# A row-lookup table moved from memory into SBUF, filled by one-hot matrix products instead of four-byte scatters

## The chip, the cores and the metric

The kernel runs on one core of a Trainium2 chip, in one launch. The metric is the device time of the whole program in microseconds (us); lower is better. A core has five engines with queues of their own. TensorE does the matrix products: PE in the profile, and PEld for the loads of its weights. VectorE (DVE), ScalarE (ACT) and GpSimd (POOL) do the rest, and SyncE (SP) only issues DMA transfers. Each engine works through its own list strictly in the order in which the program wrote it, so an instruction that waits holds up everything written behind it on that engine. SBUF is the memory on the core, PSUM the eight banks into which TensorE writes, and "memory" without a name is the chip's HBM, reached by DMA alone.

## The reference

The reference is a linear attention with two mixture-of-experts blocks behind it:

```
phi(x): p = x @ w_phi; p -= max|p|; [exp(p), exp(-p)]
attention: num = phi(q) @ (phi(k)^T v); den = phi(q) @ sum(phi(k)); num / den
block 1:   logits = x @ w_gate + bias[modality]; e = argmax; g = softmax(logits)[e]
           out = g * (relu(x @ w1[e]) @ w2[e])
block 2:   the same without the bias, and times sigmoid(x @ w_output_gate)[e]
```

There are 8 batches of 8 heads with 576 positions of 64 numbers, so 4608 rows of 512 numbers go through both blocks. Each block has 8 experts with 512 x 1024 and 1024 x 512 weights, and a row goes to one expert only.

## The kernel before, in words

**Rows and places.** A row can reach its expert only once its logits are known, so the kernel sorts rows by expert as it goes. Every finished row is written to a list in memory (`x1_d` for block 1; the code counts it as block 0). The row's place in the order of its expert is its expert's number times 4608 plus its rank among the rows of that expert so far. A table with one entry per place (8 x 4608 = 36,864 entries) says which row stands there. Later, a tile of 128 consecutive places is looked up in the table, and its 128 rows are fetched by one indirect DMA (`gather`, L749).

**The table.** It lies in memory, in five copies `tab0_0` to `tab0_4` of four-byte entries (L71), zeroed in the attention stage (`zeros`, L436). For each 128 rows `enter` (L364) issues one indirect DMA on POOL that scatters 128 entries of four bytes. Block 1 of the code (the second block of experts) has four such copies and the same `enter`.

**The attention stage.** A loop of 78 steps (L1560) treats one group of heads of one batch per step, nine steps to a batch; this text calls nine steps a period and numbers its steps 0 to 8. A step works on several batches at different stages, so that products of TensorE lie beside maxima and differences on DVE and exponentials on ACT. `weave` holds chains of small DVE instructions, from which a step takes a few at fixed points. Within a step, TensorE gets in this order: projections (`proj`, L1205), `q_less` (L1340), `kv_head` (L1297), `num` (L1382), then for rows that are nearly done `x_logits` (L376) and `a_T` (transposes, L371). `num` has one PSUM bank. Before the next `num` can write, DVE must have taken the last one out (`norm`, L1362 to L1366).

A batch's rows are stored (`x_store`), ranked on TensorE (`x_ranks`), placed on DVE (`x_places`) and entered (`x_enter`, L1529) while the loop works two periods further on. This falls in steps 6 to 8 of the period; batches with an odd number come a step later than those with an even number, and go into the table at step 0 of the next period. Even batches have 4 tiles of 128 rows here, odd ones 5.

**The turn to the experts.** The expert with most rows in the first six batches begins early. `early_rows` (L557) reads three tiles of table entries for it by DMA on SP, `early_idx` (L567) adds up the five copies on DVE, and three gathers follow. The last two batches are finished behind the loop, between the first products of the experts (`tiles()`). Then `route_a` (L614) reads the whole table into SBUF on SP, works out on DVE which tile goes to which expert, and `route_b` (L691) looks up the rows of the other 40 tiles by 30 products with a selection matrix (5 copies x 2 halves x 3 parts, L699). Memory that the attention's last rows used is used again by `route_a`; it must wait for their store.

**The experts.** 40 tiles per block, two layers per tile (`first`, L782 to L784; `second`, L802 to L806), weights loaded by SP. The rows of block 1 enter its own table four tiles at a time.

Of the kernel before, what the change touches and what calls it, by code (L numbers as in the profile page):

```python
# [53 lines left out]
def attention_two_moe(  # L54
# [13 lines left out]
    x2_d = dpool.tile([NSLOT * 128 + 1, XW], F32, name="x2_d")  # L68
    rows_of = [C1 * 128, NSLOT * 128]

    tab_d = [[dpool.tile([NROW, 1], F32, name=f"tab{n}_{k}") for k in range(K)] for n, K in enumerate((5, G))]  # L71

    whole = ((0, 1),)

# [36 lines left out]
    row_no = []  # L111
    for n in range(2):
# [6 lines left out]
        row_no.append(t.rearrange("p c t -> p (c t)").bitcast(F32))  # L119

    nxt = [iota(f"nxt{n}", [[NT, NE]]) for n in range(2)]
    row0 = iota("row0", [[NT, NE]])
# [219 lines left out]
    def places(ps, oh16, C, n, valid=None):  # L342

        pl = sp.tile([128, CM, NE], F32, tag="pl", name="pl")[:, 0:C]
        nc.vector.tensor_tensor(
            pl, ps[:, 0:C], nxt[n].unsqueeze(1).to_broadcast([128, C, NE]), op=ALU.add)
        nc.vector.tensor_tensor(nxt[n], nxt[n], ps[:, C], op=ALU.add)
        yield
        nc.vector.tensor_tensor(pl, pl, oh16[:, 0:C], op=ALU.mult)
        yield  # L350
        po = sp.tile([128, CM], F32, tag="po", name="po")[:, 0:C]
        nc.vector.tensor_reduce(out=po, in_=pl, op=ALU.add, axis=AX.X)
        yield
# [8 lines left out]
        return pi  # L362
# [155 lines left out]
    etab = [const.tile([128, len(tab_d[n]), E], F32, name=f"etab{n}") for n in range(2)]  # L518
    ereg = {}

    def early(n):
# [45 lines left out]
    def early_idx(n):  # L567
        s = sp.tile([128, E, 2], F32, tag="es", name="es")
        nc.vector.tensor_reduce(
            out=s, in_=etab[n].rearrange("p k c -> p k c").bitcast(F16).rearrange("p k (c t) -> p c t k", t=2),  # L570
            op=ALU.add, axis=AX.X)
        yield
        nc.vector.scalar_tensor_tensor(
            out=s[:, :, 1], in0=s[:, :, 0], scalar=128.0, in1=s[:, :, 1], op0=ALU.mult, op1=ALU.add)
        yield
        nc.vector.tensor_scalar(eidx[n], s[:, :, 1], float(rows_of[n]), None, op0=ALU.add)
        yield
# [12 lines left out]
    def rt(n, name, shape, dt=F32, keep=False):  # L590
        if (n, name) not in rts and keep:
            rts[n, name] = const.tile(shape, dt, name=f"{name}{n}")
        elif (n, name) not in rts:
            words = int(np.prod(shape[1:])) * (2 if dt == F16 else 4) // 4
            area = next((a for a in spare if a[1] + words <= a[2]), None)
            if shape[0] == 128 and n == 0 and area:
                rts[n, name] = view(area[0], dt, area[1] * (2 if dt == F16 else 1), *shape[1:])
                area[1] += words
            elif n == 1 and (0, name) in rts:
                rts[n, name] = rts[0, name]  # L600
            else:
                rts[n, name] = state["late"].tile(shape, dt, tag=name, name=name)
        return rts[n, name]
# [87 lines left out]
    def route_b(n):  # L691


        tab16, sel, ntile, ex = routed[n, "a"]
        rows = state["pg"][:, 3, 0 : 2 * M].rearrange("p (t m) -> p t m", t=2)
        for x in range(2):
            for i, t in enumerate(tab16):
                for k in range(3):
                    nc.tensor.matmul(  # L699
                        rows[:, x], t[:, k, :, x], sel[:, k], start=(i == 0 and k == 0),  # L700
                        stop=(i == len(tab16) - 1 and k == 2))
        rs = rt(n, "rs", [128, M])
        nc.vector.tensor_scalar(rs, rows[:, 0], 128.0, float(rows_of[n]), op0=ALU.mult, op1=ALU.add)
        idx = rt(n, "idx", [128, M], I32, True)
        nc.vector.tensor_tensor(idx, rs, rows[:, 1], op=ALU.add)
# [412 lines left out]
    with ExitStack() as actx:  # L1118
# [405 lines left out]

        def x_places(b):
            n = 4 + b % 2
            rows[b, "pi"] = yield from places(rows[b, "rk"], rows[b, "oh"], n, 0)

        def x_enter(b):  # L1529
            pi = rows.pop((b, "pi"))  # L1530
            for c in range(4 + b % 2):
                enter(0, pi, c, 9 * (b // 2) + 4 * (b % 2) + c)

        def x_store(b):
            for c, r in rows[b]:
# [19 lines left out]
        def tiles():  # L1555
            if not chains.get("route"):
                chains["route"] = next(experts)

        chains = {}
        for t in range(9 * B + 6):  # L1560
            b, s = t // 9, t % 9

            def at(lag, n=9):

                u = t - lag
                return (u // 9, u % 9) if 0 <= u < 9 * B and u % 9 < (n if n else 4 + u // 9 % 2) else None
# [35 lines left out]
            if b + 2 < B and s in (5, 6):  # L1602
                load_qk(q_of(b + 2), qT[b + 2], s - 5)
            split_step(split0, weave, t, "load")
            ready = batch_at(23)
            if ready != B - 3:
                ready = batch_at(24)
                ready = None if ready == B - 3 else ready
            if ready is not None:
                weave.finish(chains.pop(("finish", ready)))  # L1610
                x_store(ready)
# [54 lines left out]
            for x in firsts[t][1:] if 4 <= t < 9 else []:  # L1666
                proj(q_proj(*x))
                q_max(*x)
            each(5, num)
            if at(18, 0) and at(18)[0] < B - 1:  # L1670
                x_logits(*at(18))
            if at(17, 0) and at(17)[0] < B - 1:
                a_T(*at(17))
            if ready is not None:
                x_ranks(ready)
                chains["places", ready] = weave.add(x_places(ready))
# [18 lines left out]
            entered = ready if ready == B - 3 else batch_at(26)  # L1695
            if entered is not None and (entered, "pi") in rows:
                x_enter(entered)
# [6 lines left out]
            if t == 9 * B + 1:  # L1704
                done(early_idx(0))
                for i in range(E):
                    gather(0, i)
            if t in (9 * B + 1, 9 * B + 5):
# [41 lines left out]
        x_enter(last)  # L1750


    late = ctx.enter_context(tc.tile_pool(name="late", bufs=1))
# [85 lines left out]
```

## Time and profile before

| what | us |
|---|---|
| three runs: median (lowest to highest) | 1561.77 (1560.21 to 1566.68) |
| the profiled execution's own time | 1563.24 |
| its span, first to last instruction | 1561.5 |
| PE busy | 1467.9 (94%) |
| DVE busy | 746.4 (48%) |
| ACT busy | 553.4 (35%) |
| POOL busy | 228.3 (15%) |

The span is cut into 40 slices of 39 us; in the rows below a digit is the busy share of a slice in tenths, and PEclk is the granted clock of TensorE in tenths of 2.4 GHz. The attention stage takes slices 0 to 13, the two blocks of experts the rest. A wait named "issue" is one in which the profile shows nothing that the engine waited for.

### The profile page before, as it was taken

How to read it: one execution, taken by the hardware profiler on the slowest of the kernel's cores; microseconds unless marked ns; L12 is line 12 of the kernel's file. 1: busy time of each engine (PE TensorE's matmuls, PEld its weight loads, DVE VectorE, ACT ScalarE, POOL GpSimd, SP SyncE). 2: the span in 40 equal slices, each digit the busy share in tenths (PEclk: the TensorE clock that was granted, in tenths of full speed). 3: DMA queues.
4: the chain of work that ended last, by engine and by line, in shares of the span. 5: the costliest groups of instructions: out<-in, count | busy, mean ns of one | idle time of the engine just before them, and what ended most of it. 6: DMA issues, size and time to landing. Idle time of an engine off the chain costs nothing. (4 is left out here: it accounts for less than half of the span.)

```text
span 1561.5 us, 38909 instructions
## 1 busy us (share of the span) xinstructions
PE 1467.9 (94%) x15626; PEld 1157.4 (74%) x15626; DVE 746.4 (48%) x2255; ACT 553.4 (35%) x850; POOL 228.3 (15%) x273
## 2 busy tenths in 40 slices
PE   6999998987999879999999999799889999999998
PEld 4999998987989847667777776466657777777775
DVE  3668776757756434646665666354341111111111
ACT  1346565554555403334444444243211111111111
POOL 1000101101011121202211211120131211211221
PEclk8999998989989889999999999899999999999999
DMA  8255656677431753657667777678945353484381
GB/s 250 92 159 164 142 170 157 174 168 136 124 62 49 265 84 114 158 185 201 204 213 178 195 180 230 113 199 244 306 150 174 76 150 104 133 272 138 81 281 43
DMA packets 158268, 254.40 MB, mean 163 GB/s; under 512 B 90953, under 2 KB 95613, under 8 KB 152192
## 3 DMA queue, kind: packets, MB, share of 16 engines
q1 hardware_dynamic: 141264, 210.22, 50.2%
q0 software_dynamic: 14784, 41.44, 7.9%
q8 instruction: 127, 2.08, 0.7%
q14 instruction: 61, 0.50, 0.1%
q10 hardware_dynamic: 2032, 0.16, 0.1%
HBM read 428.60 MB, written 83.22 MB: 328 GB/s over the span
## 5 line engine op out<-in xcount | busy, mean ns | idle before, releaser
L784 PE MATMUL proj<-xT,w 128*128 128x128 f16 x896 | 154.8, 221 | 10.4 <-issue 10.4
L783 PE MATMUL proj<-xT,w 128*128 128x128 f16 x896 | 154.7, 221 | 6.1 <-issue 6.1
L782 PE MATMUL proj<-xT,w 128*128 128x128 f16 x896 | 154.6, 220 | 3.2 <-issue 3.2
L802 PE MATMUL num<-w,qs 128*128 128x512 f32 x336 | 151.6, 605 | 0.0
L794 DVE SCALAR_TENSOR_TENSOR qs<-proj,qs 128x512 f16<-128x512 f32 x54 | 37.4, 692 | 228.3 <-ACT qs L793 228.3
L784 PEld LDWEIGHTS <-w 128*128 128x128 f16 x1344 | 132.2, 98 | 18.6 <-issue 18.6
L802 PE MATMUL num<-ks,qs 128*128 128x512 f32 x304 | 140.1, 614 | 4.2 <-DMA ks<-in_moe_w_dram 4.2
L1382 PE MATMUL num<-kvsb,E 128*128 128x65 f32 x1024 | 129.6, 282 | 11.9 <-DVE xt L1366 11.8
L782 PE MATMUL proj<-xT,v 128*128 128x128 f16 x816 | 138.7, 219 | 0.7 <-DVE xT L771 0.7
L784 PE MATMUL proj<-xT,v 128*128 128x128 f16 x816 | 138.7, 219 | 0.2 <-issue 0.2
L783 PE MATMUL proj<-xT,v 128*128 128x128 f16 x816 | 138.7, 219 | 0.0
L782 PEld LDWEIGHTS <-w 128*128 128x128 f16 x1344 | 132.1, 98 | 8.4 <-issue 4.4
L1382 PEld LDWEIGHTS num<-kvsb,E 128*128 128x128 f32 x1024 | 125.6, 200 | 14.9 <-issue 8.3
L1297 PE MATMUL kv<-v,kp 128*128 128x128 f32 x1024 | 135.7, 288 | 0.5 <-issue 0.5
L783 PEld LDWEIGHTS <-w 128*128 128x128 f16 x1344 | 132.1, 98 | 4.0 <-issue 2.0
L752 POOL DMA_INDIRECT xg<-x_d,idx x74 | 77.6, 1049 | 388.7 <-PE px L371 189.5
L1297 PEld LDWEIGHTS kv<-v,kp 128*128 128x128 f32 x1024 | 126.6, 201 | 1.6 <-issue 1.6
L783 PEld LDWEIGHTS <-v 128*128 128x128 f16 x1216 | 118.9, 98 | 3.1 <-issue 1.0
L782 PEld LDWEIGHTS <-v 128*128 128x128 f16 x1216 | 118.9, 98 | 2.5 <-issue 0.4
L784 PEld LDWEIGHTS <-v 128*128 128x128 f16 x1216 | 118.9, 98 | 0.0
L802 PEld LDWEIGHTS num<-w,qs 128*128 128x128 f32 x336 | 63.3, 193 | 72.0 <-issue 72.0
L1205 PE MATMUL proj<-wps,ks 64*128 64x128 f32 (+1 forms) x640 | 113.9, 301 | 0.9 <-issue 0.6
(328 smaller groups left out, 3366.7 us busy)
## 6 DMA issues: line engine op xcount, KB each, us to landing
w<-pl SPq DMA_DIRECT2D x114, 1024.0 KB
v<-pl SPq DMA_DIRECT2D x80, 1024.0 KB
ks<-in_moe_w_dram SPq DMA_DIRECT2D x40, 1024.0 KB
ks<-pl SPq DMA_DIRECT2D x40, 1024.0 KB
w<-in_moe_w_dram SPq DMA_DIRECT2D x38, 1024.0 KB
wf<-in_moe_w_dram SPq DMA_DIRECT2D x64, 512.0 KB
pl<-wo SPq DMA_DIRECT2D x52, 512.0 KB
w<-in_moe_w_dram SPq DMA_DIRECT2D x32, 512.0 KB
```

The lines of the kernel that those rows point to most:

```text
L752: nc.gpsimd.indirect_dma_start(out=xg(n, i), out_offset=None, in_=src[n][0:nr, :], in_offset=bass.IndirectOffsetOnAxis(ap=ix, axis=0), bou ...
L782: nc.tensor.matmul(h[:, j], wk[:, 0, cs], xT[:, k], start=(k == 0), stop=False)
L783: nc.tensor.matmul(h[:, j], wk[:, 0, cs], xT[:, 4 + k], start=False, stop=False)
L784: nc.tensor.matmul(h[:, j], wk[:, 1, cs], xT[:, k], start=False, stop=(k == 3))
L794: nc.vector.scalar_tensor_tensor(out=lo, in0=h, scalar=0.0, in1=hi, op0=ALU.max, op1=ALU.subtract)
L802: nc.tensor.matmul(y, h[:, k], wk, start=(k == 0), stop=(k == 7))
L1205: nc.tensor.matmul(*a, **kw)
L1297: nc.tensor.matmul(ps[:, half, h % 2], kp[:, c, half, :], vw(v1, 4 * h + c), start=(h % 2 == 0 and half == 0 and c == 0), stop=False)
L1382: nc.tensor.matmul(ps[:, c, 0:V], e[:, half, 128 * c : 128 * c + 128], kw(g, half), start=(half == 0), stop=(half == 1))
```

## The change

The table of the first block of experts becomes one tile in SBUF, `tab0`: 96 partitions x 3 x 128 entries of float16. Nothing of it goes to memory: the five copies, the DMAs that zero them, the 36 scatters, the five reads of `early_rows` and the five of `route_a` go away. The second block's tables stay as they are.

For each tile of 128 rows `hots` makes two one-hot matrices on DVE: `a` (128 x 128: the low seven bits of the place, times a code for the row's number) and `o` (128 x 288: the other bits). `tab_add` multiplies them: three products per tile, summed in one PSUM bank over the 4 or 5 tiles of a batch. `tab_out` adds the bank to `tab0`. A lookup is three products (`tab_pick`) and three DVE instructions (`decode`). In the loop, all batches up to the sixth are now ready at step 6 and entered at step 7; one-hot matrices lie in buffers borrowed from other uses. In step 1, `num` is now issued behind `x_logits` and `a_T`. `early_sel` and `tab_pick` at the steps 71 and 72 replace the reads of `early_rows`, and the early gathers come one step earlier.

```diff
+    tab0 = const.tile([96, 3, 128], F16, name="tab0")
+    nc.gpsimd.memset(tab0, 0.0)
...
+        nc.vector.tensor_scalar(pi, pi, 127, None, op0=ALU.bitwise_and)
+        nc.vector.tensor_copy(pk, pi)
+        nc.vector.tensor_tensor(po, po, pk, op=ALU.subtract)
...
+    def hots(at_, pk, po, c0, mems):
+        for c, m in enumerate(mems):
+            a, o = m[:, 0:128], m[:, 128:416]
+            nc.vector.tensor_scalar(
+                a, iota128, pk[:, c : c + 1], code[:, c0 + c : c0 + c + 1], op0=ALU.is_equal, op1=ALU.mult)
+            nc.vector.tensor_scalar(o, iota_c, po[:, c : c + 1], None, op0=ALU.is_equal)
+            out_.append((a, o))
+            yield
+    def tab_add(tag, hs_):
+        ps = bank(tag, F32, 3, 128)
+        for k in range(3):
+            for i, (a, o) in enumerate(hs_):
+                nc.tensor.matmul(
+                    ps[0:96, k], o[:, 96 * k : 96 * k + 96], a, start=(i == 0), stop=(i == len(hs_) - 1))
+    def tab_out(ps):
+        nc.vector.tensor_tensor(tab0, tab0, ps[0:96], op=ALU.add)
...
-        for k, t in enumerate(tab_d[n]):          # early_rows, route_a: n = 0 has no copies left
...
+        if n == 0:                                  # route_b
+            tab_pick(rows[:, 0], sel)
+            done(decode(idx, rows[:, 0], "bits", M))
...
-            ready = batch_at(23)
-            if ready != B - 3:
-                ready = batch_at(24)
-                ready = None if ready == B - 3 else ready
+            ready, entered = [(t - x) // 9 if (t - x) % 9 == 0 and 0 <= (t - x) // 9 < B - 2 else None for x in (24, 25)]
...
-            each(5, num)
+            if entered is not None:
+                weave.finish(chains.pop(("hots", entered)))
+                x_enter(entered)
+                tab_out(rows.pop((entered, "pt")))
+            if s != 1:
+                each(5, num)
             ...
+            if s == 1:
+                each(5, num)
...
-        x_enter(last - 1)
-        tiles()
         for c in range(n):
             x_logits(last, c)
+        done(x_hots(last - 1))
+        x_enter(last - 1)
+        tab_out(rows.pop((last - 1, "pt")))
+        tiles()
         done(finish(last))
         tiles()
         x_ranks(last)
         x_store(last)
         done(x_places(last))
-        x_enter(last)
+        done(x_hots(last))
+        x_enter(last, "num2")
+        tab_out(rows.pop((last, "pt")))
```

## Rows read from the trace of the kernel before

**Rows 1.** The page: busy time of each engine (us, share of the span, instructions).
```profile
PE 1467.9 (94%) x15626; PEld 1157.4 (74%) x15626; DVE 746.4 (48%) x2255; ACT 553.4 (35%) x850; POOL 228.3 (15%) x273
```

**Rows 2.** Windows: length, busy PE PEld DVE ACT POOL (instructions), clock, DMA share, GB/s.
```profile
133.96:191.02 57.06, 54.84 (x650) 52.52 (x646) 45.53 (x120) 33.27 (x57) 4.59 (x5) 0.97 0.66 164
191.02:248.79 57.77, 55.40 (x673) 52.28 (x670) 44.00 (x119) 35.01 (x59) 5.26 (x6) 1.00 0.67 196
248.79:311.36 62.57, 58.06 (x643) 55.01 (x643) 45.34 (x120) 32.30 (x55) 5.16 (x5) 0.92 0.61 136
311.36:377.61 66.25, 60.15 (x665) 56.94 (x663) 46.77 (x127) 34.23 (x58) 6.15 (x7) 0.90 0.68 172
377.61:442.99 65.38, 56.27 (x634) 53.45 (x633) 43.44 (x118) 33.69 (x58) 4.29 (x5) 0.90 0.60 101
442.99:453.50 10.51, 8.79 (x84) 8.31 (x82) 4.72 (x14) 4.94 (x8) 0.00 (x0) 0.84 0.08 7
```

**Rows 3.** Waits of PE, 120 to 575 us: total, times, longest.
```profile
PE num L1382 <- DVE xt L1366: 10.5, 11, 2.5
PE proj L1205 <- issue: 8.3, 4, 7.4
PE proj L783 <- issue: 6.1, 3, 4.5
```

**Rows 4.** Windows during and behind two groups of scatters, columns as in rows 2.
```profile
365.00:374.00 9.00, 9.00 (x107) 8.86 (x106) 8.63 (x30) 5.97 (x10) 3.42 (x5) 1.00 0.99 326
377.00:390.00 13.00, 6.06 (x65) 5.60 (x66) 5.21 (x13) 5.07 (x8) 0.00 (x0) 0.78 1.13 48
...
555.00:566.00 11.00, 3.87 (x57) 3.04 (x53) 5.51 (x26) 0.69 (x1) 3.58 (x4) 0.81 1.07 27
```

**Rows 5.** DMA queues, 376 to 392, then 360 to 374 us: packets, MB, share.
```profile
q8 instruction: 1, 0.02, 4.2%
...
q8 instruction: 1, 0.02, 0.4%
```

**Rows 6.** Line 365, the scatters: duration ns min/median/max, first and last start us.
```profile
L365 POOL DMA_INDIRECT tab<-row_no,pi x76: 967/974/1502, 178.3 to 1145.5; - x76
```

**Rows 7.** Window of one step 6, columns as in rows 2.
```profile
172.03:177.93 5.90, 4.99 (x50) 4.58 (x49) 5.83 (x19) 2.55 (x4) 0.00 (x0) 0.85 1.02 345
```

**Rows 8.** DVE groups by line: count, busy us, mean ns of one, idle before.
```profile
L1274 DVE TENSOR_TENSOR kd<-proj,km 128x512 f32<-128x512 f32 x72 | 49.0, 681 | 0.2
L360 DVE CAST pi<-po 128x5 int32<-128x5 f32 x4 | 0.7, 170 | 0.2
```

**Rows 9.** Line 123, a 128x128 comparison on DVE: duration ns min/median/max.
```profile
L123 DVE TENSOR_SCALAR tri<-iota,iota_p x1: 283/283/283, 13.3 to 13.3; 128x128 f16<-128x128 f32 x1
```

**Rows 10.** Timeline, turn to the experts: start, length, instruction, count, idle before.
```profile
500.79 10.80 SPq L562 DMA_DIRECT2D etab<-tab  x5
...
516.70 2.90 PE L1382 MATMUL num<-kvsb,E 128*128 128x65 f32 x16 [2.50 <-DVE xt L1366]
...
554.67 0.27 PE L339 MATMUL pl<-oh,ones 128*128 128x40 f16 x5
...
571.30 0.49 DVE L657 TENSOR_TENSOR lt<-v,v 128x320 f32<-128x320 f32 x1 [9.94 <-DMA x_d<-kvsb]
...
572.37 0.61 PE L371 MATMUL px<-ident,qs 128*128 128x128 f16 x8
572.81 7.09 PE L802 MATMUL num<-w,qs 128*128 128x512 f32 x16
...
583.67 2.91 PE L802 MATMUL num<-w,qs 128*128 128x512 f32 x3
```

**Rows 11.** Windows behind the early lookup and behind the lookup, columns as in rows 2.
```profile
517.50:531.20 13.70, 13.70 (x114) 12.96 (x114) 4.60 (x19) 3.23 (x6) 2.25 (x5) 0.50 1.02 394
582.40:589.20 6.80, 6.42 (x28) 3.21 (x29) 3.76 (x16) 0.69 (x1) 2.49 (x3) 0.50 0.86 298
```

**Rows 12.** Waits of PE, 600 to 1100 us: total, times, longest.
```profile
PE proj L784 <- issue: 9.6, 1, 9.6
```

More of the change, by code (lines that the diff above doesn't have):

```diff
@@ L69, in attention_two_moe @@
     rows_of = [C1 * 128, NSLOT * 128]
-    tab_d = [[dpool.tile([NROW, 1], F32, name=f"tab{n}_{k}") for k in range(K)] for n, K in enumerate((5, G))]
+    tab_d = [[dpool.tile([NROW, 1], F32, name=f"tab{n}_{k}") for k in range(K)] for n, K in enumerate((0, G))]
     whole = ((0, 1),)
@@ L109, in attention_two_moe @@
     nc.gpsimd.iota(col_no, [[96, 3]], base=1, channel_multiplier=1, allow_small_or_imprecise_dtypes=True)
-    row_no = []
-    for n in range(2):
+    row_no = [None]
+    for n in (1,):
         nc_ = rows_of[n] // 128
@@ L517, in attention_two_moe @@
     eidx = [const.tile([128, E], I32, name=f"eidx{n}") for n in range(2)]
-    etab = [const.tile([128, len(tab_d[n]), E], F32, name=f"etab{n}") for n in range(2)]
+    etab = [None, const.tile([128, len(tab_d[1]), E], F32, name="etab1")]
     ereg = {}
@@ L565, in early_rows, with early_sel, tab_pick, early_idx @@
                     "e (c p) -> p (e c)", p=128))
[L567 to L572, printed above, removed]
-        nc.vector.scalar_tensor_tensor(
[L574 to L577, printed above, removed]
+    def early_sel():
+        ec = sp.tile([128, E], F32, tag="ec", name="ec")
+        nc.vector.tensor_scalar(ec, iota_m[:, 0:E], 1.0, None, op0=ALU.add)
+        nc.vector.scalar_tensor_tensor(
+            out=ec, in0=eno[0][:, 0:1].to_broadcast([128, E]), scalar=float(C1), in1=ec, op0=ALU.mult, op1=ALU.add)
+        sel = sp.tile([96, 3, E], F16, tag="esel", name="esel")
+        nc.vector.tensor_tensor(
+            sel, ec[0:96].unsqueeze(1).to_broadcast([96, 3, E]), col_no.unsqueeze(2).to_broadcast([96, 3, E]),
+            op=ALU.is_equal)
+        return sel
+    def tab_pick(ps, sel):
+        for k in range(3):
+            nc.tensor.matmul(ps, tab0[:, k], sel[:, k], start=(k == 0), stop=(k == 2))
+    def early_idx(n, ps=None):
+        if n == 0:
+            yield from decode(eidx[0], ps, "ebits", E)
+        else:
+            s = sp.tile([128, E, 2], F32, tag="es", name="es")
+            nc.vector.tensor_reduce(
+                out=s, in_=etab[n].rearrange("p k c -> p k c").bitcast(F16).rearrange("p k (c t) -> p c t k", t=2),
+                op=ALU.add, axis=AX.X)
+            yield
+            nc.vector.scalar_tensor_tensor(
+                out=s[:, :, 1], in0=s[:, :, 0], scalar=128.0, in1=s[:, :, 1], op0=ALU.mult, op1=ALU.add)
+            yield
+            nc.vector.tensor_scalar(eidx[n], s[:, :, 1], float(rows_of[n]), None, op0=ALU.add)
+            yield
         nc.vector.tensor_tensor(wes[n], winv[:, n, 0], winv[:, n, 1], op=ALU.mult)
@@ L695, in route_b @@
         rows = state["pg"][:, 3, 0 : 2 * M].rearrange("p (t m) -> p t m", t=2)
[L696 to L703, printed above, removed]
-        idx = rt(n, "idx", [128, M], I32, True)
-        nc.vector.tensor_tensor(idx, rs, rows[:, 1], op=ALU.add)
+        idx = rt(n, "idx", [128, M], I32, True)
+        if n == 0:
+            tab_pick(rows[:, 0], sel)
+            done(decode(idx, rows[:, 0], "bits", M))
+        else:
+            for x in range(2):
+                for i, t in enumerate(tab16):
+                    for k in range(3):
+                        nc.tensor.matmul(
+                            rows[:, x], t[:, k, :, x], sel[:, k], start=(i == 0 and k == 0),
+                            stop=(i == len(tab16) - 1 and k == 2))
+            rs = rt(n, "rs", [128, M])
+            nc.vector.tensor_scalar(rs, rows[:, 0], 128.0, float(rows_of[n]), op0=ALU.mult, op1=ALU.add)
+            nc.vector.tensor_tensor(idx, rs, rows[:, 1], op=ALU.add)
         nti = rt(n, "nt", [1, 1], I32, True)
@@ L1526, in x_places, with x_hots, x_enter @@
             n = 4 + b % 2
[L1527 to L1532, printed above, removed]
+            rows[b, "pk"] = yield from places(rows[b, "rk"], rows[b, "oh"], n, 0)
+        def x_hots(b):
+            n = 4 + b % 2
+            if b < B - 2:
+                areas = [wk.tile([128, 4 * F], F32, tag="kd", name="kd"),
+                         wk.tile([128, 8, 128], F16, tag="xT", name="xT", bufs=1).rearrange("p a b -> p (a b)")]
+            else:
+                areas = [io.tile([128, 4, 2, F], F32, tag="kprem", name="kprem", bufs=1).rearrange("p a b c -> p (a b c)")]
+            mems = []
+            for a in areas:
+                a = a if a.dtype == F16 else a.bitcast(F16)
+                mems += [a[:, 416 * i : 416 * i + 416] for i in range(a.shape[1] // 416)]
+            mems = mems[0:4]
+            if n == 5:
+                mems.append(sm.tile([128, 416], F16, tag="hot", name="hot", bufs=1))
+            at_ = []
+            pk, po = rows.pop((b, "pk"))
+            yield from hots(at_, pk, po, 9 * (b // 2) + 4 * (b % 2), mems)
+            rows[b, "hots"] = at_[0]
+        def x_enter(b, tag="qf"):
+            rows[b, "pt"] = tab_add(tag, rows.pop((b, "hots")))
         def x_store(b):
@@ L1694, in attention_two_moe @@
                 weave.finish(chains.pop(("places", ready)))
-            entered = ready if ready == B - 3 else batch_at(26)
-            if entered is not None and (entered, "pi") in rows:
-                x_enter(entered)
+                chains["hots", ready] = weave.add(x_hots(ready))
+                weave.step(2)
             if t == 9 * B - 3:
@@ L1703, in attention_two_moe @@
                 early_rows(0)
-            if t == 9 * B + 1:
-                done(early_idx(0))
+            if t == 9 * B - 1:
+                esel = early_sel()
+            if t == 9 * B:
+                ps = p_small[:, 384 : 384 + E]
+                tab_pick(ps, esel)
+                done(early_idx(0, ps))
                 for i in range(E):
```

26 lines of the change are left out of this document (25 added, 1 removed).

## The prediction

> **What bounds the kernel now.** I read the page first. TensorE is busy 94% of the span [rows 1], so the reader should look for time in which it is idle, or busy at half speed. I went on to windows, one for each period of nine steps in the attention stage [rows 2]. The first two take 57.06 and 57.77 us at a clock of 0.97 and 1.00. The next three do nearly the same work in 62.57, 66.25 and 65.38 us at 0.90 to 0.92. The third view, the waits of TensorE, says what the idle time is: 8.3 us before projections and 6.1 us before `first`, put down to "issue", and 10.5 us in 11 waits of `num` for DVE [rows 3].
>
> "Issue" means that no semaphore was waited for, so I looked at DMA. During one group of scatters the DMA engines moved 326 GB/s at a share of 0.99; right behind it they were as busy (1.13) and moved 48 GB/s, and behind a later group 27 GB/s at 1.07 [rows 4]. Busy engines that move little mean that single packets take long. One of those packets fetches instructions: the single fetch between 376 and 392 us took 4.2% of 16 engines x 16 us = 10.8 us, where one between 360 and 374 took 0.4% of 16 x 14 us = 0.9 us [rows 5]. TensorE then waited 7.4 us for "issue" [rows 3], and the clock fell [rows 2]. Scatters begin at 178 us [rows 6], and of the four periods behind them one is not hurt (57.77), three are [rows 2]. So I read: a group of four-byte scatters slows all DMA behind it; where an instruction fetch falls into that stretch it comes too late, TensorE stands, and then works on at a granted 0.50, 1.2 GHz [rows 11].
>
> [...]
>
> **The change part by part**, against the profiled execution of 1563.2 us (span 1561.5; 1.5 us above the median of 1561.8).
>
> *Slow DMA in the attention stage.* Three long periods against the mean of the first two (57.4): 194.2 - 172.2 = 22.0 us [rows 2]. Step 0 of the next period has 10.51 - 8.79 = 1.7 us idle and 16% of its clock missing, 1.7 us more: 3.4. All this follows scatters that go away: **-25**. If stalls have other causes, none of it goes; with the shorter waits behind it, up to -29.
>
> *Step 1.* `num` is now behind `x_logits` and `a_T`, which TensorE can do while DVE finishes `xt`. Of 10.5 us in 11 waits [rows 3], six steps 1 have about 1 us each, and 8 transposes alone take 0.61 us [rows 10]: **-4** (0 to -6). The transposed rows are ready: DVE wrote them before `xt`.
>
> *TensorE's new work.* 36 tiles x 3 products. Eight transposes of that size take 0.61 us [rows 10], 0.06 to 0.08 each: 81 in the loop and 12 behind it cost 5.2 us at 0.056 (7 at 0.076), on the path because TensorE is it: **+5**. The last 15 are in the turn, below. 30 lookup products become 3.
>
> *DVE's new work.* Per period three small instructions of 0.17 [rows 8]; per tile `a`, a 128x128 comparison (0.28, back to back some 0.2 [rows 9]) and `o`, 288 numbers: no more than 0.49, the float32 one of 320 numbers [rows 10], no less than a small one's 0.17 [rows 8]. I take 0.55 for both, between 0.35 and 0.75, as float16 from and to SBUF isn't in the trace. `tab_out` adds 384 numbers from PSUM, 0.68 for 512 [rows 8], so 0.5. Together 0.5 + 4.5 x 0.55 + 0.5 = 3.5 us a period, in steps 6 and 7. [...]
>
> DVE has 57.06 - 45.53 = 11.5 us free in a period, 1.3 a step [rows 2], but in one step 6 it is busy 5.83 of 5.90 us, and TensorE idle 0.9 [rows 7]. Odd batches now also finish and rank a step earlier, into the same step 6. What queues behind: `k_max`, `k_sub` and `norm` of the next step, and TensorE waits for these, with one bank for `num`. Two steps hide some 2 us, so 1.5 us come through, and at half clock behind part of these gaps 0.3 more: 1.8 x 6 = **+11** (0 to +30). The products of step 7 wait for `hots` themselves.
>
> *Scatters and zeros.* 36 of 76 scatters of 0.97 us leave POOL [rows 6], where they delayed nothing on the path; setup gains a memset, two iotas and four small DVE instructions and loses three, under 1 us before the first loads: 0. Five stores of zeros leave SP.
>
> *Early tiles.* The five reads of `early_rows` held SP for 10.80 us [rows 10], with the first expert weights behind them. DVE stood for them, then TensorE 2.50 us, and 16 products took 2.90 us behind it, at the lower clock. Now `tab_pick` is three products on numbers in SBUF. 2.5 go for sure. From 517.5 to 531.2 the clock is 0.50 with TensorE busy throughout [rows 11], which costs up to 6.8 us; I take half, as TensorE is little loaded just before: **-6** (0 to -9). Weights come earlier, which nothing waits for.
>
> *The turn.* Before: ranks end at 554.9; `first` is torn apart by slow fetches (4.5 us in one [rows 3]); `route_a` on DVE waits 9.94 us for the store of the last rows, to 571.30; transposes, `second` from 572.81, then the lookup, and the next product at 583.67 [rows 10]. After: behind the ranks come about eight small DVE instructions (1.5), five tiles of one-hots (2.75) and 15 products (1.1), with TensorE idle: 560.3. Then 96 products of `first` at 0.056, 5.4 us, 2 us for a lower clock, 0.6 of transposes, 7.1 of `second`, 0.6 for logits and three products: 576.0 instead of 583.7, **-7.7**. `route_a` starts 4 us later but no longer waits for a slow store. The half clock behind the lookup's wait (6.42 us busy at 0.50 [rows 11]) gives **-3.2**. Together -11 (-5 to -15).
>
> *Sum:* -25 - 4 + 5 + 11 - 6 - 11 = -30, so 1533; against the median **1532 us**. The experts of block 1 keep their 40 scatters of the other table, and one wait of 9.6 us for "issue" [rows 12]; other instruction counts shift the fetches against these slow stretches, by 10 us either way.
>
> **The rivals.**
>
> 1. *DVE absorbs the new work*, and the lower clock goes with the stalls: `o` is fast (for that speaks that free time is there on the average [rows 2], against it the full step 6 [rows 7]). Then +11 becomes +1 and the turn and the early tiles give -24: 1563.2 - 25 - 4 + 5 + 1 - 24 = 1516; with luck in the second table's stalls 1506.
> 2. *The "issue" waits aren't the scatters'.* Stores of rows share each period with them, and the fetch may be late for its own reasons; against it, full speed during the scatters and 48 GB/s right behind [rows 4]. Then -25 falls away, and of the turn only the lookup's wait goes, some 6 us, against 4 us of new wait for one-hots: 1563.2 - 4 + 5 + 11 - 6 - 2 = 1567.
> 3. *Slower: TensorE waits for `hots` in step 7 of six periods.* The other terms give 25 + 4 - 5 + 6 + 11 = 41 us, so it decides from 6.8 us a period on. Price: one-hots at 0.75 and small instructions make 4.4, the finish of odd batches adds 2, and a lower clock behind each gap 2.5, as the step behind [rows 7] at 0.85 shows it begins: 9 x 6 = 54, so 1576.
>
> **How the numbers follow.** Forecast (1517 to 1548) 0.63, rival 1 0.22, rival 2 0.07, rival 3 0.08. Range: 1504 to 1557, which takes in rival 1 and the forecast with DVE at +25; the likeliest's own is 1517 to 1548. What this kernel's runs can tell from no change is about 0.5%, 8 us. Faster by more: 0.63 + 0.22 + a little of rival 3 = 0.86; within: 0.05; slower: 0.09.
>
> **What would show it.** Right: periods of 57 to 60 us all through, GB/s that doesn't fall between 245 and 560 us, waits of TensorE for "issue" gone there, `lt` not waiting for the store, the product behind the lookup near 557 in place of 584. Step 7 shows the cost: `num` or the 96-column products waiting for DVE. Wrong: a fall of GB/s behind stores alone, or steps 6 and 7 longer by more than 6 us.

## The result, and the profile after it

| what | before | after |
|---|---|---|
| median of the runs on one chip, us | 1564.22 (1560.21 to 1567.72, 4 runs) | 1537.38 (1537.06 to 1538.08, 4 runs) |
| ratio | | 0.986 (95%: 0.981 to 0.991) |
| the profiled execution, its span | 1563.24, 1561.5 | 1537.06, 1535.2 |

The forecast was 1532 us in a range of 1504 to 1557. The time lies in it, but the sum behind it does not hold: a gain where it was forecast came out as a loss, and a part that was put at zero came out as a gain. The stages show it. Boundaries are the last `k_max` of the attention loop, the first product of `second` (first early tile), the product behind the lookup, the 65th product of `second` (two tiles later) and the 641st (the end of block 1).

| stretch of the profiled execution | before | after | difference | forecast |
|---|---|---|---|---|
| start to the last `k_max` | 499.7 | 504.7 | +4.9 | -13 (-25 - 4 + 5 + 11) |
| to the first early tile's `second` | 48.0 | 50.4 | +2.4 | -6 |
| to the product behind the lookup | 36.0 | 25.0 | -11.0 | -7.7 |
| to the 65th product of `second` | 36.7 | 34.0 | -2.7 | -3.2 |
| to the 641st | 513.2 | 489.6 | -23.6 | 0 (10 either way) |
| to the end | 427.9 | 431.6 | +3.7 | 0 |

The page, and the periods of the attention stage (length, busy PE PEld DVE ACT POOL with counts, clock, DMA share, GB/s), answer to [rows 1, 2]:

```profile
PE 1467.3 (96%) x15710; PEld 1162.3 (76%) x15710; DVE 770.2 (50%) x2365; ACT 552.4 (36%) x850; POOL 193.5 (13%) x239
```

```profile
132.07:194.70 62.63, 57.97 (x662) 54.97 (x658) 48.02 (x132) 33.14 (x57) 0.35 (x1) 0.95 0.54 167
194.70:257.61 62.91, 59.02 (x682) 55.90 (x678) 47.43 (x132) 34.55 (x59) 0.35 (x1) 0.95 0.52 162
257.61:320.94 63.33, 59.12 (x662) 55.98 (x658) 47.91 (x131) 32.47 (x56) 1.25 (x1) 0.92 0.48 149
320.94:386.67 65.73, 59.40 (x682) 56.11 (x678) 50.03 (x140) 35.35 (x59) 1.08 (x2) 0.95 0.50 155
386.67:449.75 63.08, 58.59 (x648) 55.41 (x645) 45.89 (x129) 32.37 (x57) 0.35 (x1) 0.92 0.32 100
```

All five are as long as the disturbed ones of before. The first two, which had taken 57.06 and 57.77 us, are 5 us longer. The cause is not the old one. The waits of PE in the stretch of [rows 3] have no "issue" left:

```profile
PE qf L402 <- DVE kd L394: 12.3, 10, 2.6
PE num L1460 <- DVE xt L1444: 10.3, 11, 2.5
PE num L402 <- DVE kprem L394: 2.7, 4, 2.1
PE qf L402 <- DVE xT L394: 1.6, 8, 0.2
```

The DMA rows of 240 to 560 us follow, in 40 slices of 8 us (busy share in tenths, then GB/s), first before, then after. Before, slices 9 and 10 are 7 and 8 tenths busy and move 31 and 57 GB/s, and the last is at 9 tenths and moves 67: that is the slow DMA. After, every slice of 8 or 9 tenths moves 197 GB/s or more.

```profile
DMA  9094924978765906898650076410101400899409
GB/s 306 2 123 92 250 96 150 322 31 57 187 139 132 342 16 226 289 62 71 168 146 21 2 266 116 20 66 2 66 2 48 186 2 1 308 404 397 180 2 67
```

```profile
DMA  6418651914319909332770060101102409990302
GB/s 267 147 62 214 142 205 69 348 58 139 133 52 197 311 3 316 125 97 110 202 178 5 6 261 1 68 2 66 68 2 84 152 0 334 408 388 25 120 18 96
```

What is late now is seen in one step 7, in the timeline of PE (start, length, instruction, count, idle before) and, below it, of DVE:

```profile
176.41 0.61 PE L1380 MATMUL kv<-v,kprem 128*128 128x130 f32 x4
179.60 0.26 PE L402 MATMUL qf<-kd 128*96 128x128 f16 x1 [2.58 <-DVE kd L394]
180.06 0.26 PE L402 MATMUL qf<-kd 128*96 128x128 f16 x1 [0.20 <-DVE kd L394]
...
181.41 0.28 PE L402 MATMUL qf<-xT 128*96 128x128 f16 x2
181.53 1.51 PE L1460 MATMUL num<-kvsb,E 128*128 128x65 f32 x8
```

```profile
177.54 0.41 DVE L1444 TENSOR_TENSOR xt<-num,den 128x256 f32<-128x256 f32 x1
...
179.01 0.34 DVE L392 TENSOR_SCALAR kd<-iota,pk,code 128x128 f16<-128x128 f32 x1
179.26 0.28 DVE L394 TENSOR_SCALAR kd<-iota_c,po 128x288 f16<-128x288 f16 x1
179.47 0.34 DVE L392 TENSOR_SCALAR kd<-iota,pk,code 128x128 f16<-128x128 f32 x1
...
181.73 0.55 DVE L407 TENSOR_TENSOR tab<-tab,qf 96x384 f16<-96x384 f16 x1 [0.80 <-PE qf L402]
```

The products (L402) stand ahead of `num` in TensorE's list. `num` could have started at 177.95, when `xt` was out; it starts at 181.53, and from 181.9 us on TensorE works at half clock (granted 0.50) for 6.8 us. Four of the six periods have this wait, of 2.55 to 2.58 us, the last one a shorter one (1.04); in the second 2.52 us stand ahead of `num` in the step before, where DVE is full with the odd batch (10.6 us busy in the 12.1 up to 236.56). A stretch at 0.50, of 6.8 to 13.7 us, follows each of the six.

The turn came as forecast. TensorE waits for the last one-hot matrices, `lt` on DVE starts at 573.0 us without a wait for the store, and the lookup is three products without a wait [rows 10]:

```profile
564.41 0.26 PE L402 MATMUL num<-kprem 128*96 128x128 f16 x1 [2.10 <-DVE kprem L394]
...
572.84 7.09 PE L880 MATMUL num<-w,qs 128*128 128x512 f32 x16
...
579.97 0.23 PE L636 MATMUL qf<-ks,tab 96*128 96x40 f16 x3
580.04 1.96 PE L880 MATMUL num<-w,qs 128*128 128x512 f32 x4
```

Among the experts of block 1 the wait of 9.6 us [rows 12] is gone; these are the waits of PE in the same stretch:

```profile
PE proj L861 <- issue: 1.9, 1, 1.9
PE kv L860 <- issue: 1.7, 1, 1.7
PE kv L862 <- issue: 1.1, 1, 1.1
```

### The profile page after: what moved, and what is told of

Read it like the earlier page. It is cut to its first block, busy times and chain, and to the rows that moved or that the text cites. A ratio compares the mean times of both kernels' runs of the same rounds, so it can differ in the third digit from the quotient of the medians.

```text
span 1535.2 us, 39035 instructions
## 1 busy us (share of the span) xinstructions
PE 1467.3 (96%) x15710; PEld 1162.3 (76%) x15710; DVE 770.2 (50%) x2365; ACT 552.4 (36%) x850; POOL 193.5 (13%) x239
## 5 line engine op out<-in xcount | busy, mean ns | idle before, releaser
L1460 PE MATMUL num<-kvsb,E 128*128 128x65 f32 x1024 | 135.2, 289 | 12.5 <-DVE xt L1444 11.6
L1460 PEld LDWEIGHTS num<-kvsb,E 128*128 128x128 f32 x1024 | 131.1, 207 | 15.3 <-issue 10.0
L880 PE MATMUL num<-ks,qs 128*128 128x512 f32 x304 | 134.6, 596 | 0.0
```

The source lines that it names most:

```text
L880: nc.tensor.matmul(y, h[:, k], wk, start=(k == 0), stop=(k == 7))
L1460: nc.tensor.matmul(ps[:, c, 0:V], e[:, half, 128 * c : 128 * c + 128], kw(g, half), start=(half == 0), stop=(half == 1))
```

## The experiments

Twelve kernels ran, in three groups of four; each group shared the runs of the kernel before, whose median was 1551.82 us (25 runs, 1540.29 to 1559.50), 1550.05 (17 runs) and 1562.83 (11 runs). The first two groups ran on one chip, the third on another; 1 to 3 below are the first group, 4 to 7 the second, 8 to 10 the third. Ratios are to these. Times are medians of several executions, stages and waits are read from one profiled execution of each kernel. For the attention stage, **loop** is the time from the first `k_max` of the third period to the last `k_max`: 365.8 us before, 372.6 after. It is the sum in a row of windows over six periods.

**1. The scatters put back into the changed kernel.**

```diff
+            x_scatter(late_)      # 4 or 5 x enter() into spare_d[c], which nothing reads
```

> The changed kernel with the 36 scatters of the first table put back beside the products, into five spare tables in memory that nothing reads, at the places where the kernel before had them. Theory 1 (the scatters slow all DMA behind them, and instruction fetches that fall into these stretches come late): GB/s falls again right behind each group between 180 and 580 us, TensorE waits for 'issue' there again, and the attention stage gets longer by about the 22 us by which the three long periods of the kernel before exceeded its first two; time 1553 us (1545 to 1570). Rival (the late fetches came from the loads and stores that share the period, or from where the code lay, not from the scatters): the scatters cost POOL alone, which is idle there, and the time stays at 1537 us, within 4.

Measured: 1557.83 us, ratio 1.002 (0.999 to 1.006). The waits for "issue" return (5.4 us in one), but the loop is 381.7 us, only 9.1 longer than after (14.3 longer than in experiment 5), where the time is 22 us above experiment 5's on the same chip; the rest lies behind the loop, 6.7 us of it ahead of the product behind the lookup and 7.3 among the experts of block 1. The end agrees with theory 1, the place does not, so a cleaner kernel was needed (experiments 4 and 6).

**2. The products behind `num`.**

```diff
-            if entered is not None:
-                weave.finish(chains.pop(("hots", entered)))
-                x_enter(entered)
-                tab_out(rows.pop((entered, "pt")))
             if s != 1:
                 each(5, num)
+            if entered is not None:
+                weave.finish(chains.pop(("hots", entered)))
+                x_enter(entered, "px")
...
             split_step(split0, weave, t, "lo")
+            if entered is not None:
+                tab_out(rows.pop((entered, "pt")))
```

> The changed kernel, but in step 7 the products with the one-hot matrices stand behind num instead of ahead of it, in the bank px, which is free there, and tab_out stands at the end of the step. Theory 1 (TensorE loses time in step 7 because these products, ahead of num in its order, wait for DVE to make the last one-hot matrices, while num and the next step stand behind them): the six gaps of 1.0 to 2.6 us ahead of them shrink below 1 us, the half clock behind them goes in most periods, step 7 falls from 11.8 to 12.9 us to about 9 to 10; time 1520 us (1512 to 1529). Rival (DVE is the bound in steps 6 and 7, busy 10.79 of 11.79 us in the first of them): the wait moves to num of the next step or to projections, the two steps together stay as long, and the time stays at 1537 us, within 4.

Measured: 1505.08 us, ratio 0.972 (0.968 to 0.977). The same step 7, and the loop:

```profile
176.76 1.97 PE L1460 MATMUL num<-kvsb,E 128*128 128x65 f32 x16 [1.08 <-DVE xt L1444]
178.57 0.42 PE L402 MATMUL px<-kd 128*96 128x128 f16 x2
179.19 0.26 PE L402 MATMUL px<-xT 128*96 128x128 f16 x1 [0.20 <-DVE xT L394]
```

```profile
sum 346.83, PE 329.51 PEld 312.60 DVE 274.15 ACT 197.22 POOL 3.39; mean PE 54.92 PEld 52.10 DVE 45.69 ACT 32.87 POOL 0.57
```

DVE does the same (7.04 us busy in this step against 7.22), the step takes 7.20 us instead of 11.79, and the loop is 25.7 us shorter than after and 20.5 shorter than in experiment 5, a second execution of the changed kernel. Theory 1 holds; its price of 17 us was too low. Four of the six periods keep a wait of 1.05 to 1.08 us; the clock fell behind one of these.

**3. Instruction fetches shifted**, in the changed kernel and in the one before.

```diff
+        for _ in range(64):
+            nc.tensor.matmul(ps[:, 0:8], ones16, ones16[:, 0:8], start=True, stop=True)
```

> The changed kernel with 64 tiny products (128x8) more in the warm-up, before the first loads have landed, so that every later instruction of TensorE lies 128 places further on; the trace shows one instruction fetch for 256 instructions of TensorE, so that is half the distance between two fetches. Theory 1 (which fetch meets which slow stretch decides the waits for 'issue' in block 1's experts, and so chance of position gave a part of the gain): the attention stage stays as it is within 3 us, the waits for 'issue' between 600 and 1125 us stand at other places and sum to another value, the time moves by 3 to 20 us, most likely up, 1547 us. Rival (these waits belong to places of the program, such as a table read or the end of a stage): same places, same sum, 1537 us plus at most 3 for the products themselves.

> The kernel before with the same 64 tiny products in the warm-up. Theory 1 (position of fetches against slow stretches): the long waits for 'issue' (7.4, 4.5, 3.7, 3.5 and 9.6 us) leave their places and others appear, in the attention stage and among the experts; the time moves by 3 to 20 us in either direction, 1545 to 1580. Rival (the waits belong to places of the program): same waits at the same instructions, 1564 us within 4.

Measured: 1545.63 us, ratio 0.996 (0.994 to 0.998), and 1556.70, ratio 1.003 (0.999 to 1.006). In the changed kernel the loop (374.9) and the turn stay, and the waits for "issue" among the experts move: 3.9 us at 869 and 3.4 at 983. In the kernel before all long waits stand elsewhere: 6.7 us at 311, 4.2 at 390, 4.0 at 935 and none of 9.6 among the experts. Its loop is 369.4 us, 3.6 longer than before, and its time does not move clear of noise, where 3 to 20 us were expected. So position decides which stretch is hit: 128 instructions cost the changed kernel 0.8% against experiment 5, and the intervals do not overlap.

**4. The kernel before without the 36 scatters.**

```diff
     def enter(n, pi, c, r):
+        if n == 0:
+            return
```

> The kernel before without the 36 scatters of the first table, everything else as it was. Left out is the filling of the table, so that the experts' rows are not the reference's (early tiles read row 0, the others an empty row, and no row of block 2 counts); only the attention stage, up to the last k_max at 499.7 us in the kernel before, is to be compared. Prediction's step (-25 us with the scatters): the slow stretches and the waits for 'issue' go, all periods are near 57.4 us, and the last k_max stands at 475 us (472 to 479). Rival (the 7.8 us by which the attention loop grew when the scatters were put back into the changed kernel, 512.7 against 504.8): last k_max at 492 us (488 to 496).

Measured in one execution: last `k_max` at 466.5 us. The loop and the waits of PE in it:

```profile
190.93:247.00 56.07, 54.21 (x667) 51.79 (x663) 43.97 (x118) 34.73 (x59) 0.35 (x1) 1.00 0.58 181
...
304.20:359.80 55.60, 54.06 (x667) 51.71 (x663) 46.54 (x126) 35.56 (x59) 0.72 (x2) 1.00 0.59 184
...
sum 332.60, PE 321.42 PEld 307.22 DVE 257.00 ACT 198.32 POOL 3.01; mean PE 53.57 PEld 51.20 DVE 42.83 ACT 33.05 POOL 0.50
```

```profile
PE num L1384 <- DVE xt L1368: 13.2, 15, 1.7
```

"Issue" is gone from the list, and the loop is 33.1 us shorter (332.7 us from `k_max` to `k_max`; the first window above starts 0.06 us late), or 36.7 shorter than with the fetches of the kernel before shifted. Not even the forecast of 25 was enough, and the rival of 8 is out.

**5. The changed kernel again**, in more rounds.

> The changed kernel itself, unaltered, timed in more rounds beside the kernel before. In the profiled runs so far the stretch from the product behind the lookup to the first products of block 2 took 550 us in the kernel before and 539 with its fetches shifted, 524 in the changed kernel and 532 with its fetches shifted. Theory 1 (most of the 26 us gained stood in waits of that stretch, which chance of position decides, and not in the attention stage): the attention loop's last k_max stands near 504.7 us again, as it is not touched by chance, and the whole differs from the kernel before by less than the 1.4% of the first comparison, about 0.5 to 1.0%. Rival (the gain belongs to the change): 0.986 again, within 0.003.

Measured: 1535.82 us, ratio 0.988 (0.983 to 0.992). The rival holds: the gain repeats, though it is 14 us here and was 27 in the first comparison, where the kernel before was slower (1564.22 against 1550.05). The last `k_max` came at 497.9, not at 504.7 (loop 367.4): one of the waits was 1.0 us instead of 2.57. From the 65th to the 641st product of `second` it took 489.4 us, as after.

**6. The scatters put back into the version of experiment 2.** The edit is that of experiment 1.

> The version with the products behind num (1505.1 us, last k_max at 477.6 us), with the 36 scatters put back into five spare tables that nothing reads, at the places where the kernel before had them. Theory 1 (a scatter group costs what the prediction said, and the long waits in step 7 of the changed kernel had only hidden a part of it, as the slow stretch passed while TensorE stood or ran at half clock anyway): the attention loop grows by 18 to 25 us, last k_max at 496 to 502; time 1527 us (1518 to 1535). Rival (a group costs little, as 7.8 us in the first trial showed): last k_max at 485 us, time 1514 us (1508 to 1517).

Measured: 1549.66 us, ratio 0.999 (0.995 to 1.003).

```profile
sum 363.86, PE 339.40 PEld 322.12 DVE 275.38 ACT 196.12 POOL 30.26; mean PE 56.57 PEld 53.69 DVE 45.90 ACT 32.69 POOL 5.04
```

```profile
PE num L1462 <- DVE xt L1446: 17.2, 14, 2.5
PE qf L1285 <- issue: 2.1, 1, 2.1
PE num L1462 <- issue: 1.5, 2, 1.3
PE proj L1285 <- issue: 1.5, 1, 1.5
```

The loop is 17.0 us longer than in experiment 2, nearer to theory 1 than to the rival's 7.8; last `k_max` at 495.6. What the same scatters cost a loop was thus 33.1, 17.0 and 9.1 us. Theory 1 would have it that they cost less where TensorE stands for other reasons; no run separates that from where the fetches happened to fall. Only the first was measured in the program that the forecast spoke of. The total grew by 44.6 us, more than expected; the rest lies behind the loop: in the profiled executions 9.3 us between the lookup and the 65th product, where TensorE waits from 574.7 us on for gathered rows (the line below), and 8.8 among the experts of block 1.

```profile
PE pl L428 <- DMA xg<-x_d,idx: 7.0, 1, 7.0
```

**7. `num` of step 1 put back** ahead of `x_logits` and `a_T`, in the version of experiment 2.

> The version with the products behind num (1505.1 us), with num of step 1 put back ahead of x_logits and a_T, where the kernel before had it. Prediction's step (-4 us for this part, six steps with about 1 us of wait each): TensorE waits for DVE xt ahead of num in step 1 again, about 1.1 to 1.3 us in six periods, last k_max 4 us later at 481.6 us, time 1509 us (1507 to 1512). Rival (the wait is only moved: x_logits and a_T behind num let DVE catch up later in the step): last k_max within 1 us of 477.6, time 1505 us, within 2.

Measured: 1516.27 us, ratio 0.974 (0.969 to 0.980).

```profile
sum 353.55, PE 335.61 PEld 319.81 DVE 274.96 ACT 198.46 POOL 3.39; mean PE 55.94 PEld 53.30 DVE 45.83 ACT 33.08 POOL 0.57
```

The loop is 6.7 us longer, and the time is above the expected 1507 to 1512. Step 1 takes 5.62 us against 4.98 in three periods, with a wait of 1.31 us; in two others the clock is 0.50 behind the wait, and the step takes 6.9 and 7.1. The first is a cost of the order; the second, half clock, comes and goes between runs of one kernel (the third and fourth of the six periods had a clock of 0.94 and 1.00 in experiment 2, of 1.00 and 0.92 in experiment 10), so that the forecast's 4 and the 6.7 do not contradict each other.

**8. What about a scatter is slow?** Into the version of experiment 2 came 36 scatters of 512-byte rows, or 36 plain stores of 128 neighbouring four-byte entries.

```diff
-    spare_d = [dpool.tile([NROW, 1], F32, name=f"spare{k}") for k in range(5)]
+    spare_d = [dpool.tile([NROW, 128], F32, name=f"spare{k}") for k in range(5)]
...
-            in_=row_no[n][:, r : r + 1], in_offset=None, bounds_check=NROW - 1, oob_is_err=False)
+            in_=row_no[n][:, r : r + 1] if n else iota128, in_offset=None, bounds_check=NROW - 1, oob_is_err=False)
```

> As the trial with the scatters put back into the version with the products behind num, but each of the 36 scatters writes 128 rows of 512 bytes in place of 128 entries of four bytes, at the same places of a table that nothing reads. The stretch from the first k_max of the third period to the last one took 346.9 us without scatters and 363.9 with those of four bytes. Theory 1 (what slows the DMA is that single entries of four bytes are written): no slow stretch behind the groups, 347 to 350 us, time 1505 us (1502 to 1513). Rival (any scatter of 128 rows to far places does it): 360 us or more, GB/s falls behind each group, time 1530 to 1550.

```diff
+        if n == 0:
+            nc.gpsimd.dma_start(out=spare_d[c][128 * r : 128 * r + 128, :], in_=row_no[0][:, r : r + 1])
+            return
```

> The same with 36 plain stores of 128 x 4 bytes to neighbouring places in memory, issued by POOL where the scatters stood: four-byte pieces, but no scattered places and no indices. Theory 1 (the size of the pieces): slow stretches behind each group as with the scatters, 358 to 366 us from the third period's first k_max to the last, time 1530 to 1550. Rival (the scattered places matter): 347 to 350 us, time 1505 us (1502 to 1513).

Measured: 1527.61 us, ratio 0.978 (0.973 to 0.983), and 1546.80, ratio 0.988 (0.983 to 0.993). The loop with the wide scatters:

```profile
sum 349.54, PE 330.95 PEld 314.36 DVE 275.00 ACT 196.35 POOL 30.22; mean PE 55.16 PEld 52.39 DVE 45.83 ACT 32.73 POOL 5.04
```

With the plain stores, the stretch behind one group, the loop, and the waits of PE:

```profile
385.00:396.00 11.00, 2.45 (x34) 2.04 (x32) 4.66 (x9) 0.31 (x2) 0.00 (x0) 0.78 1.03 99
```

```profile
sum 382.30, PE 345.69 PEld 328.41 DVE 274.72 ACT 196.72 POOL 17.87; mean PE 57.62 PEld 54.74 DVE 45.79 ACT 32.79 POOL 2.98
```

```profile
PE num L1465 <- DVE xt L1449: 14.1, 13, 2.5
PE qf L1288 <- issue: 8.6, 1, 8.6
PE proj L1288 <- issue: 6.6, 2, 5.2
PE kv L1380 <- issue: 4.4, 1, 4.4
```

In the loop theory 1 holds on both sides: rows of 512 bytes cost 3.3 us against experiment 10 (346.2), plain stores of four bytes 36.1, more than the 12 to 20 expected, with DMA at a share of 1.03 and 99 GB/s while TensorE is busy 2.45 of 11 us. (POOL waited 16 us for earlier ones of its stores.) Of the two sizes tried, four bytes slowed the DMA in these runs and 512 did not; the scattered places were not needed for it. The time of the wide scatters was missed: 1527.6, 16 us above experiment 10, most of it again behind the loop.

**9. `o` on POOL**, in the version of experiment 2.

```diff
-            nc.vector.tensor_scalar(o, iota_c, po[:, c : c + 1], None, op0=ALU.is_equal)
+            nc.gpsimd.tensor_scalar(o, iota_c, po[:, c : c + 1], None, op0=ALU.is_equal)
```

> The version with the products behind num, with the matrices o (128x288) made by POOL instead of DVE; POOL has next to nothing to do in the attention stage. In the version before it, steps 5 to 8 of six periods are 21 us longer than in the kernel before without its scatters, 5 us of which are the products. Theory 1 (what is left is DVE's time): DVE gets 4.5 x 0.26 us a period back, num waits less in step 7, the stretch from the third period's first k_max to the last falls from 346.9 to 341 us, time 1499 us (1495 to 1503). Rival (POOL is slower at it than DVE and the products wait for POOL, or DVE's instructions beside POOL's take longer): 346 to 353 us, time 1505 to 1512.

Measured: 1515.41 us, ratio 0.970 (0.965 to 0.974); loop 346.7. One `o` takes 1.00 us on POOL against 0.29 on DVE:

```profile
L394 POOL TENSOR_SCALAR kd<-iota_c,po x12: 997/1003/1052, 171.9 to 466.2; 128x288 f16<-128x288 f16 x12
```

Nothing is won in the loop: three periods are 0.6 to 1.3 us shorter than in experiment 10 and the other three longer, two of these with more half clock. The waits of 1.07 us ahead of `num` stay: they are waits for `xt`, which stands ahead of the one-hot matrices in DVE's list. The rival holds.

**10. The version of experiment 2 again.**

> The version with the products behind num, unaltered, in more rounds, as the reference for the other three on the same chip: 1505 us (1502 to 1510), 0.972 of the kernel before within 0.004, and 346.9 us within 2 from the third period's first k_max to the last.

Measured: 1511.34 us, ratio 0.966 (0.962 to 0.969), loop 346.2. The loop is as expected; the time is 1 us above the expected range and the ratio below its own, on a chip where the kernel before is 11 us slower. It beats both kernels, on two chips: 0.972 and 0.966 of the kernel before, where the changed kernel has 0.986 and 0.988.

## Why the time came out where it did, step by step

**Slow DMA in the attention stage (-25).** The mechanism was right, the size too small. Without the scatters the loop is 33.1 us shorter and no wait for "issue" is left. The mean of the first two periods (57.4) was taken as undisturbed; without scatters the second takes 56.07 and the fourth 55.60 us (experiment 4).

That "issue" is a late fetch is seen twice more. In the kernel before, the fetch of 10.8 us ended at 389.7 and TensorE went on at 390.6; another of 6.4 us ended at 449.3, and a wait of TensorE with it. In the loops of experiments 1, 6 and 8 there are five waits for "issue" of over 2 us (5.4, 2.1, 5.2, 8.6 and 4.4), and all five come at the same place in a block of 256: behind the 7873rd, 3777th, 5825th, 7873rd and 8897th record of TensorE in the trace, weight loads included, each of which leaves 193 when divided by 256. The trace has about one fetch for 256 of these records (127 for 31,610 in experiment 6), so it looks like the place where a new block begins. In the kernel before only the shortest of five waits, 1.1 us, stands at that place. And in the three experiments the fetch packet next to the wait took only 0.9 to 2.9 us itself; next to the waits of 3.7 us at 316.6 and of 9.6 us [rows 12] in the kernel before no slow fetch is seen. So what a late fetch waits for is not shown.

**Step 1 (-4).** Right, as far as it was measured: experiment 7, in another version, gives 6.7 us with half clock behind two of the waits, and about 0.65 us in each of five periods without it.

**TensorE's new work (+5).** Products that do not wait start 0.056 us apart (eight in 0.45 us from 181.08 on), so 81 take 4.5 us, as forecast.

**DVE's new work (+11): the step that failed.** DVE's own time was put too high: a pair of `a` and `o` takes 0.46 us in a row, not 0.55, so a period has some 3.1 us of new work, not 3.5. (The trace gives one `a` 0.34 us and one `o` 0.29; their starts lie 0.25 and 0.21 us apart.) What failed is the sentence "Two steps hide some 2 us, so 1.5 us come through". It counted DVE's free time and treated the wait of the products as one more place where DVE is late. But these products stand ahead of `num`, so all that DVE has to do before the last `o` delays `num` and the whole next step. The loop after (372.6) against the loop without scatters and with `num` moved (332.6 - 6.7 = 325.9) gives 46.7 us of new cost, 41.5 in experiment 5. The stages agree: the steps 5 to 8 of the six periods are 46.6 us longer after than in experiment 4. Of it 25.7 (20.5 in experiment 5) go when the products change places with `num` (experiment 2), 4.5 are the products, and some 16 are left, which I put down to DVE's work. Much of that stands with batches 1 and 3, which now finish a step earlier: in experiment 2 the steps 5 to 8 of their periods are 4.9 and 5.2 us longer than in experiment 4. No experiment takes this part away by itself, so it is argued, not shown.

This is rival 3, which had 0.08. Without the 4.5 of the products it cost 42 us, 7.0 us a period (6.2 in experiment 5), about the 6.8 from which it was said to decide, and beyond the range of 0 to 30 that the term had. The kernel was not slower, because the scatters gave 33 instead of 25 and because of the experts below.

**Early tiles (-6).** Not seen in this run: +2.4. The wait of 2.5 us went, but the clock was at 0.50 all the same: from 496.0 us for 13.7 us, behind the wait of 1.04 us in the last period's step 7, and again from 523.3 for 10.2 us, with no longer wait of TensorE just before it than 0.79 us. In experiment 2, with half clock for 3.4 us alone, this stretch takes 42.7 us against 48.0 before. In experiment 10 it takes 49.2, at 0.50 for 13.7 us. So the half clock here does not hang on the lookup's wait alone, to which the forecast tied it.

**The turn (-11).** -13.8 with the stretch behind the lookup. With the gains forecast ahead of it the product behind the lookup was to come near 557; it came at 580.0, mainly because the loop was 18 us and the early tiles 8 us slower than forecast.

**The experts of block 1 (0, 10 either way).** -23.6, the largest part of the gain of 26.3 in the two profiled executions:

```profile
620.40:1133.60 513.20, 491.21 (x4945) 345.60 (x4943) 284.80 (x944) 199.72 (x261) 89.62 (x97) 0.98 0.73 199
```

```profile
614.00:1103.60 489.60, 484.55 (x4946) 342.77 (x4944) 284.54 (x944) 199.65 (x261) 89.84 (x97) 1.00 0.73 208
```

First before, then after: the same work, with the same DMA share, but 22 us of idle time in one and 5 in the other, and 7 us more of busy time in the first, which has 24 us at half clock against 3. Before, 15.5 us of the idle time are waits for "issue" and 6.0 for weights. Position is a part of it: shifted fetches gave 503.8 for the kernel before (-9.4) and 498.4 for the changed one (+8.8). Whether it is all of it stays open. All profiled kernels with the first table's scatters, wide ones included, took 497 to 513 us in this stretch, and those without any DMA in their place 488 to 498; one with plain stores took 498. The ranges hardly overlap, yet nothing in the traces shows how scatters that ended before 600 us would reach to 900. The second table's scatters run in this stretch in all of them. One run points at these: in experiment 4, where no row of block 2 counts and so their places lie past the table's end, the stretch took 482.8 us with no wait of TensorE in it. Its rows are not the reference's, so this is a pointer and no proof. What was forecast as luck of either sign was at least no part of the change's design; a range of 10 was too narrow for it.

So the forecast of 1532 was near the 1537 by luck, because two errors met: the loop was put 18 us too low, the experts 24 too high.

## What to carry to other kernels

When work is added for an engine with free time, look at the instruction that will wait for it on the other engine, and at what is queued behind that: the same work cost 20 to 26 us more ahead of `num` than behind it. Scatters of four-byte entries are to be priced by what they do to all DMA behind them, instruction fetches included, not by their own issue time of 0.97 us: here they cost the loop 33.1, 17.0 and 9.1 us. A change in the number of instructions moves the fetches, and in the changed kernel, with the 40 scatters of its second table, that alone moved the time by 0.8% (experiment 3), so a single comparison can give a stage a gain that is not the change's.

## What was not expected of the hardware

- Thirty-six plain stores of 128 four-byte entries each, 18 KB in all, lengthened the loop by 36.1 us; 36 scatters of 64 KB each lengthened it by 3.3.
- A comparison of 128x288 float16 took 1.00 us on POOL and 0.29 on DVE.
- Of 23 waits of TensorE of 2.5 to 2.6 us in the profiled attention stages, 22 had the granted clock fall to 0.50 around their end; the one that did not is in experiment 1, at 236 us. Of the four waits of 1.05 to 1.08 us in experiment 2 one had it.
